# A linear-attention layer with a two-way maxout layer on one core: all operations and loads in another order, and 90 operations on other engines

## The chip, the cores and the metric

The kernel runs on one core of a Trainium2 chip. The core has TensorE (PE in the profile, its weight loads PEld), VectorE (DVE), ScalarE (ACT), GpSimd (POOL), and SyncE (SP), whose in-order queue issues all DMAs here. The engines run side by side, each works through its own instructions in order, and semaphores tie them together. The metric is the device time of one execution in microseconds.

## The reference

Inputs are r, k, v, w of 4 batches x 8 heads x 768 tokens x 48, u of 8 x 48, and three weight matrices.

```
state = 0
for t in range(768):                      # per batch and head, state is 48 x 48
    cur   = outer(u * k[t], v[t])
    y[t]  = r[t] @ (state + cur)
    state = w[t][:, None] * state + outer(k[t], v[t])
x   = y as 3072 tokens x 384
out = maximum(x @ w1, x @ w2) @ w_out     # 384 -> 1024 -> 384
```

## The kernel before

The work is cut into eight units. `UNITS` gives each (first batch, batches, segment of 256 tokens): units 0 to 3 are one batch each in segment 0, units 4 and 5 two batches each in segment 1, units 6 and 7 two batches each in segment 2. Each partition holds two neighbouring tokens, so a segment fills 128 partitions. The steps are small functions, named in the table by name, unit and further numbers:

- `load` brings w, r, k or v of a unit. `wp` multiplies the two decays of a token pair, `ln` takes the logarithm, `ex` sums it along tokens by a matmul with a triangle (units 3 to 7 with two half-precision parts, `hi` and `lo`), `mz` adds the unit's own part, `ie` and `e0` are exponentials of the sums (ScalarE).
- `rw` and `kw` are products with the second decay; `scale.n.0` makes the scaled r (`rp`), `scale.n.1` the scaled k (`kp`). `tr` transposes both on TensorE and `te` copies them to SBUF (units 0 to 4); `dt` transposes by DMA (units 5 to 7).
- `rk`, `ru`, `dg`, `dd`, `di` make the diagonal term with u. `sc` is the score matmul, `mk` merges it under a mask into M on VectorE, `vb` casts v, `ya` applies M to v, `yi` applies the state, `kv`, `st`, `sm`, `sb` update the state, `xe` copies y to SBUF as bf16.
- The maxout is max(h1, h2) = h2 + relu(h1 - h2). `wdiff` makes w1 - w2 once (three parts), `w2turn`, `w2take`, `wfold`, `wctake` fold w2 with w_out, `wocast` casts w_out. `gt` is the matmul with the difference, `rl` its relu (ScalarE or VectorE), `op` the output matmul, `oe` copies it out, `os` stores it.
- `hot` is eight matmuls on zeros each, of no use to the result; 48 of them stand in the front of both programs. `zero`, `ident`, `tri`, `mask` and `identb` fill constants.

What sets the order is one table, `ORDER`: a loop goes through it and calls the function of each word, so each engine's instructions stand in the table's order, and SyncE's queue too. Letters behind an @ choose the engine of a step (a for ScalarE, d for VectorE, p for GpSimd). `mul` (L176 on VectorE, L180 on GpSimd) makes one instruction of a product on VectorE and two halves on GpSimd; `copy` is L168. The tiles have few buffers (PSUM: four banks of tag G, two pairs of tag Y), which are handed on in the table's order.

```python
    for o in ORDER:
        o, _, e = o.partition("@")
        name, *a = o.split(".")
        a = [int(x) if x.isdigit() else x for x in a] + ([e] if e else [])
        if name in ops:
            ops[name](*a)
        else:
            unit[name](U[a[0]], *a[1:])
```

Of the kernel before, what the change touches and what calls it, by code (L numbers as in the profile page):

```python
# [59 lines left out]
rw.1.0@d wt.1.0 wload.1.2 ln.2.0 ex.2.0 vb.0.0@a we.0.1 scale.0.0.0.0@d zero.k.0@d kv.0  # L60
scale.0.0.0.1@d tr.0.0.1 dd.0@p mz.2.0 woload.0 we.1.0 ru.1.0@p kw.1.0@p row.2 w2turn.0.0 e0.1.0
scale.1.0.0.0@d st.0.0@a tr.0.0.0 te.0.0.1@a sc.0.0.1.1 sc.0.0.0.1 w2turn.0.1 dg.1 te.0.0.0@a
w2take.0.0@a wload.0.2 load.2.v scale.1.1.0.0@d dd.1@p sb.0.0@a wp.3.0@p tr.1.0.1 e0.2.0 st.0.1
te.1.0.1@a rk.2.0@d zero.M.2@p di.0.0@d ie.2.0 zero.M.0@p rw.2.0@d hot.8.1 wload.1.1 ru.2.0@d
kw.2.0@p scale.2.1.0.0@p sc.0.0.1.0 sc.0.0.0.0 mk.0.0.1.0 vb.1.0@a hot.8.4 mk.0.0.0.0 mk.0.0.1.1
mk.0.0.0.1 vb.1.1@a kv.1 scale.2.0.0.0@d tr.1.0.0 ln.3.0 te.1.0.0@a w2turn.2.1 wdiff.2@p sb.0.1@a
st.1.0@a sb.1.0@a di.1.0@d st.1.1 tr.2.0.0 w2take.0.1@a tr.2.0.1 te.2.0.1@a zero.v.0@d sc.1.0.1.0
w2turn.1.0 wload.0.0 wdiff.0@p w2take.1.0@a sc.1.0.0.0 mk.1.0.1.0 mk.1.0.0.0 sb.1.1@a w2take.2.1@d
w2turn.2.0 w2turn.1.1 w2take.2.0@a hi.3@a ya.0.0.1.0 vb.2.1@a ya.1.0.0.0 sm.0@p sm.1@p wload.0.1
wdiff.1@d ya.1.0.1.0 ya.0.0.0.1 load.3.r trih@a yi.1.0 yi.0.0 ya.0.0.0.0 woload.1 ya.0.0.1.1  # L70
xe.1.0@a xe.0.0@d load.3.k te.2.0.0@a gt.1.3 rl.1.3@a dg.2 rk.3.0@d lo.3@d dd.2@a gt.0.2 rl.0.2@a
wocast.1@p gt.1.1 w2take.1.1@d woload.3 gt.0.0 rw.3.0@p woload.2 rl.0.0@a gt.1.2 load.4.w.0 rl.1.2@a
vb.2.0@p ru.3.0@p gt.0.3 rl.0.3@a ex.3.0 wocast.3@d wocast.2@a wocast.0@a rl.1.1@a di.2.0@d
sc.2.0.1.0 mk.2.0.1.0 gt.0.1 mz.3.0 e0.3.0 kw.3.0@p gt.1.0 dg.3 sc.2.0.0.0 kv.2 st.2.0@a rl.0.1@a
wp.4.0@d ie.3.0 scale.3.0.0.0@d mk.2.0.0.0 wfold.2 sb.2.1@d wfold.0 dd.3@p ln.4.0 load.3.v st.2.1
wfold.1 sb.2.0@d vb.3.0@a wl.2 hi.4@a lo.4@d ya.2.0.0.0 load.4.r rl.1.0@a di.3.0@d vb.3.1@a row.3
ya.2.0.1.0 wctake.1@a we.2 load.4.k wctake.2@a rk.4.0@d wctake.0@a scale.3.1.0.0@p tr.3.0.0 ex.4.0
mz.4.0 tr.3.0.1 ex.4.1 mz.4.1 te.3.0.0@a kv.3 te.3.0.1@a st.3.0@a yi.2.0 xe.2.0@d ie.4.0 op.1.1
oe.1.1@a st.3.1 load.4.v e0.4.0 sb.3.0@a ru.4.0@d gt.2.0 load.5.w.0 rl.2.0@a sc.3.0.0.0 sc.3.0.1.0
vb.4.1@a gt.2.2 op.1.0 rk.4.1@p rw.4.0@d kw.4.0@d scale.4.0.0.0@d scale.4.1.1.0@d scale.4.1.0.0@p  # L80
e0.4.1 rl.2.2@a scale.4.0.1.0@d op.0.1 sb.3.1@a row.4 oe.1.0@a tr.4.1.0 te.4.1.0@a tr.4.1.1 vb.4.0@a
op.0.0 sm.2@p wl.3 mk.3.0.0.0 ya.3.0.0.0 mk.3.0.1.0 ya.3.0.1.0 yi.3.0 oe.0.1@d ru.4.1@p wp.5.0@p
we.3 sm.3@p te.4.1.1@a gt.2.1 xe.3.0@a dg.4 ln.5.0 oe.0.0@d tr.4.0.1 te.4.0.1@a gt.3.0 rl.3.0@a
rl.2.1@a hi.5@a dd.4@d load.5.k kv.4 di.4.0@d sc.4.1.1.0 load.5.r load.5.v rk.5.0@d gt.2.3 rl.2.3@a
gt.3.2 tr.4.0.0 di.4.1@d te.4.0.0@a mk.4.1.1.0 gt.3.3 st.4.0 st.4.1 os.1.0 rl.3.3@a gt.3.1 rl.3.1@a
ru.5.0@p sc.4.1.0.0 rk.5.1@p sc.4.0.0.0 load.6.r sb.4.0@a vb.5.1@a op.2.1 load.6.w.0 lo.5@d wl.4
ex.5.0 mk.4.0.0.0 os.0.0 sb.4.1@a mk.4.1.0.0 oe.2.1@a mz.5.0 e0.5.0 rw.5.0@p ex.5.1 sc.4.0.1.0
load.6.k ru.5.1@p mz.5.1 ya.4.0.0.0 scale.5.0.0.0@d op.2.0 rl.3.2@a op.3.0 mk.4.0.1.0 e0.5.1 os.1.1
scale.5.0.1.0@d dt.5.0.0 ya.4.0.1.0 dt.5.0.1 kw.5.0@d row.5 oe.3.0@d os.3.0 wp.6.0@p ie.5.0
ya.4.1.1.0 ya.4.1.0.0 oe.2.0@d yi.4.1 xe.4.1@d dg.5 dd.5@d scale.5.1.0.0@p di.5.0@d yi.4.0 xe.4.0@a  # L90
op.3.1 rk.6.0@d ln.6.0 hi.6@d gt.4.2 rl.4.2@a lo.6@d gt.4.5 scale.5.1.1.0@p rl.4.5@a os.2.1 gt.4.0
vb.5.0@a gt.4.7 rl.4.7@a we.4 sm.4@p gt.4.4 dt.5.1.0 gt.4.6 sc.5.0.1.0 mk.5.0.1.0 kv.5 oe.3.1@a
rl.4.6@a rl.4.0@a rl.4.4@a st.5.0 gt.4.1 rl.4.1@a sc.5.0.0.0 mk.5.0.0.0 gt.4.3 rl.4.3@a dt.5.1.1
rk.6.1@p st.5.1 ex.6.0 ru.6.1@p sb.5.1@a sb.5.0@a load.6.v os.0.1 vb.6.1@a mz.6.0 ex.6.1 op.4.3
load.7.w.0 load.7.k mz.6.1 e0.6.1 ie.6.0 kw.6.0@d e0.6.0 scale.6.1.1.0@p di.5.1@d sc.5.1.0.0
ya.5.0.1.0 rw.6.0@d ya.5.0.0.0 yi.5.0 xe.5.0@a vb.6.0@a scale.6.0.0.0@d op.4.2 wl.5 os.3.1
scale.6.1.0.0@p sc.5.1.1.0 oe.4.2@a op.4.0 oe.4.3@a oe.4.0@a mk.5.1.0.0 wp.7.0@p ya.5.1.0.0
mk.5.1.1.0 dt.6.0.0 ya.5.1.1.0 yi.5.1 kv.6 scale.6.0.1.0@d dt.6.0.1 xe.5.1@d st.6.0 dt.6.1.1 ln.7.0
op.4.1 sb.6.1@a sb.6.0@a oe.4.1@a ru.6.0@d dg.6 load.7.r dd.6@p gt.5.2 rl.5.2@a gt.5.4 di.6.1@d
gt.5.6 rl.5.6@a hi.7@a gt.5.0 dt.6.1.0 rl.5.0@a gt.5.3 di.6.0@d sc.6.1.1.0 rl.5.3@d rl.5.4@a  # L100
sc.6.1.0.0 gt.5.5 rl.5.5@a os.4.1 gt.5.7 rl.5.7@a rk.7.0@p lo.7@d gt.5.1 we.5 mk.6.1.1.0 rl.5.1@a
ex.7.0 op.5.1 op.5.2 oe.5.2@a sc.6.0.0.0 mk.6.1.0.0 ru.7.0@d mz.7.0 sc.6.0.1.0 mk.6.0.1.0 rk.7.1@p
ex.7.1 mk.6.0.0.0 e0.7.0 mz.7.1 op.5.3 oe.5.1@a load.7.v vb.7.1@a sm.5@p rw.7.0@p ie.7.0 os.2.0
ya.6.0.1.0 os.5.2 os.4.0 ya.6.1.0.0 ya.6.0.0.0 oe.5.3@a os.4.3 kw.7.0@p scale.7.1.1.0@p
scale.7.0.0.0@d ya.6.1.1.0 yi.6.0 xe.6.0@a scale.7.1.0.0@d dt.7.0.0 dt.7.1.0 yi.6.1 op.5.0 vb.7.0@p
xe.6.1@a gt.6.5 oe.5.0@d os.5.0 e0.7.1 gt.6.3 rl.6.3@a rl.6.5@a scale.7.0.1.0@d dt.7.1.1 gt.6.2
dt.7.0.1 os.4.2 kv.7 gt.6.6 gt.6.0 rl.6.6@a os.5.1 st.7.0 gt.6.1 rl.6.2@a ru.7.1@p dg.7 sb.7.1@a
gt.6.7 rl.6.7@a rl.6.0@d sc.7.0.0.0 rl.6.1@a dd.7@p di.7.0@d sc.7.0.1.0 mk.7.0.1.0 mk.7.0.0.0 gt.6.4
rl.6.4@a op.6.0 sc.7.1.0.0 sb.7.0@a sc.7.1.1.0 op.6.2 di.7.1@d mk.7.1.1.0 op.6.3 yi.7.1 mk.7.1.0.0
yi.7.0 ya.7.0.0.0 oe.6.2@a ya.7.1.0.0 ya.7.1.1.0 ya.7.0.1.0 xe.7.0@d op.6.1 oe.6.3@a os.6.3 oe.6.0@d  # L110
os.5.3 os.6.2 oe.6.1@d xe.7.1@a gt.7.1 rl.7.1@d gt.7.0 gt.7.6 os.6.0 rl.7.0@a gt.7.2 gt.7.3 rl.7.2@a
rl.7.6@a rl.7.3@a os.6.1 gt.7.4 rl.7.4@a gt.7.7 rl.7.7@d gt.7.5 rl.7.5@d op.7.0 op.7.1 oe.7.0@d
# [685 lines left out]
```

## Time and profile before

| | |
|---|---|
| time, median of 3 runs | 146.14 us (146.12 to 146.55) |
| span of the profiled execution | 147.2 us |
| TensorE busy | 136.8 us, 93% |
| VectorE busy | 116.9 us, 79% |
| ScalarE busy | 90.6 us, 62% |
| GpSimd busy | 90.0 us, 61% |
| read and written in HBM | 23.61 and 4.73 MB |

The span runs from the first to the last instruction of one profiled execution; no other time of that execution is given. Groups are told by line, engine, operation and tiles, with busy time, mean duration and the idle time just before; the chain of waits goes back from the last instruction to what released it. Line numbers of the changed kernel are one higher from the table on.

### The profile page before, as it was taken

What the parts mean: (1) busy time and instruction counts of PE and PEld (TensorE: products, weight loads), DVE (VectorE), ACT (ScalarE), POOL (GpSimd) and SP (SyncE); (2) the same over time, 40 slices, a digit from 0 to 9 for tenths busy, and PEclk for the clock granted to TensorE, in tenths of its full rate; (3) what the DMA queues carried; (4) which work ended last, traced back from release to release, by engine and by line L of the source; (5) the groups of instructions that cost most, each with busy time, mean ns of one, the idle gap of its engine ahead of it and who ended that gap; (6) DMA issues with size and microseconds to landing.
All of it is one profiled execution on the core that took longest, in us unless ns stands there. A gap on an engine that the chain in (4) does not pass through costs nothing.

```text
span 147.2 us, 5536 instructions
## 1 busy us (share of the span) xinstructions
PE 136.8 (93%) x2403; PEld 84.2 (57%) x2404; DVE 116.9 (79%) x162; ACT 90.6 (62%) x164; POOL 90.0 (61%) x106
## 2 busy tenths in 40 slices
...
GB/s 104 323 325 357 335 401 394 366 286 304 214 241 277 212 226 282 312 255 174 205 192 177 292 251 207 141 138 291 250 136 78 131 271 20 0 210 62 4 56 157
DMA packets 71186, 31.84 MB, mean 216 GB/s; under 512 B 66293, under 2 KB 70390, under 8 KB 71162
## 3 DMA queue, kind: packets, MB, share of 16 engines
...
q14 instruction: 5, 0.04, 0.2%
HBM read 23.61 MB, written 4.73 MB: 193 GB/s over the span
## 4 chain that ended last, share of the span: by engine, by line
PE 41%; DVE 35%; issue 6%; POOL 6%; DMA 4%; ACT 3%; SPq 2%; DVEq 0%; POOLq 0%; ACTq 0%
PE G L729 12%; DVE M L650 9%; PE G L706 8%; PE G L234 7%; PE G L725 5%; DVE rp L176 4%; DMA lv<-in_v_dram 4%; DVE rku L176 3%; DVE dg L502 3%; POOL kp L180 3%; DVE M L516 3%; PE Y L688 2%; SPq L582 2%; POOL rku L180 2%; PE Y L675 2%
## 5 line engine op out<-in xcount | busy, mean ns | idle before, releaser
L729 PE MATMUL G<-wo_sb,gT 128*128 128x384 bf16 x192 | 35.8, 331 | 0.0
L706 PE MATMUL G<-xT,wd_sb 128*128 128x256 bf16 (+1 forms) x192 | 34.4, 326 | 0.7 <-ACT xT L168 0.6
L650 DVE CAST_PREDICATED M<-mask,Y 128x1024 bf16<-128x1024 int32 (+1 forms) x26 | 28.6, 1131 | 2.8 <-PE Y L641 1.9
L717 ACT ACTIVATE gT<-G 128x512 bf16<-128x512 f32 x43 | 24.5, 601 | 9.8 <-PE G L706 9.6
L729 PEld LDWEIGHTS <-gT 128*128 128x128 bf16 x192 | 19.0, 99 | 12.6 <-issue 0.3
L706 PEld LDWEIGHTS <-wd_sb 128*128 128x128 bf16 x192 | 17.9, 98 | 12.6 <-DVE wd_sb L176 0.6
L180 POOL TENSOR_TENSOR kp<-lk,iE 128x384 bf16<-128x384 f32 x16 | 17.1, 1096 | 9.3 <-DVE lk L176 4.2
L725 PE MATMUL G<-wc_sb,xT 128*128 128x384 bf16 x72 | 15.7, 327 | 0.0
L180 POOL TENSOR_TENSOR rku<-rku,u_b 128x384 f32<-128x384 f32 x14 | 14.5, 1053 | 2.0 <-DVE rku L176 2.0
L234 PE MATMUL G<-S_b 128*128 128x512 bf16 x47 | 13.6, 442 | 1.8 <-DVE S_b L263 1.8
L168 ACT COPY RK<-G 128x1024 bf16<-128x1024 bf16 x12 | 12.1, 1019 | 4.7 <-PE G L565 4.7
L168 ACT COPY osb<-G 128x384 f32<-128x384 f32 x7 | 3.4, 479 | 15.9 <-PE G L729 12.6
L180 POOL TENSOR_TENSOR rku<-lr,lk 128x384 f32<-128x384 f32 x8 | 10.9, 1393 | 2.5 <-DMA lk<-in_k_dram 1.7
L641 PE MATMUL Y<-RK 48*64 48x128 bf16 x384 | 9.0, 220 | 2.6 <-DVE M L650 2.4
L502 DVE TENSOR_REDUCE dg<-rku 128x16 f32<-128x768 f32 x12 | 11.0, 945 | 0.1
L641 PEld LDWEIGHTS <-RK 48*64 48x64 bf16 x384 | 6.2, 106 | 7.8 <-issue 6.7
L168 ACT CAST xT<-Y 128x768 bf16<-128x768 f32 x7 | 7.0, 1025 | 5.3 <-PE Y L675 4.0
L168 ACT CAST S_b<-S_f 64x768 bf16<-64x768 f32 (+1 forms) x14 | 8.7, 624 | 2.3 <-DVE S_f L612 2.0
L176 DVE TENSOR_TENSOR rp<-lr,G 128x768 bf16<-128x768 f32 (+2 forms) x11 | 8.8, 799 | 1.4 <-ACT G L436 1.4
L234 PEld LDWEIGHTS <-S_b 128*128 128x128 bf16 x48 | 5.1, 112 | 8.3 <-issue 3.3
L516 DVE TENSOR_TENSOR M<-identq,gd 128x512 int32<-128x512 int32 x12 | 9.2, 778 | 0.4 <-POOL gd L168 0.3
L168 DVE CAST xT<-Y 128x768 bf16<-128x768 f32 x5 | 5.1, 1017 | 5.5 <-PE Y L688 3.2
...
## 6 DMA issues: line engine op xcount, KB each, us to landing
...
```

Source lines behind the costliest of these rows:

```text
L168: (nc.scalar.copy if e == "a" else nc.vector.tensor_copy if e == "d" else nc.gpsimd.tensor_copy)(o, i)
L176: op(o, a, b)
L180: op(o[:, g], a[:, g], b[:, g])
L234: nc.tensor.matmul(t, zz[:, 0:P], zz[:, 0:512], start=True, stop=True)
L502: nc.vector.reduce_sum(s.dg[:, b].rearrange("p i h -> p h i"), s.rku[:, b], axis=AX.X)
L516: (nc.vector if en == "d" else nc.gpsimd).tensor_tensor(out=o, in0=m, in1=g.unsqueeze(3).to_broadcast([P, 2, H, Q // 2]), op=ALU.bitwise_and)
L641: nc.tensor.matmul(t[q * Q:(q + 1) * Q, e, p * P:(p + 1) * P].rearrange("s (i g) -> s i g", i=2), s.kT[d, b, j, y * n + p, q, :], s.rT[d, ...
L650: nc.vector.copy_predicated(t[:, :, 2 * n * y:2 * n * (y + 1)].rearrange("s i (p e) g -> s p e i g", e=2), mask[:, j].bitcast(I32).unsquee ...
L706: nc.tensor.matmul(t[:, m * n * P:(m + 1) * n * P].rearrange("c (b t) -> c b t", t=P), wd_sb[:, ko, fo * P:(fo + 1) * P], s.xT[:, 0:n, ko, :],
L717: nc.scalar.activation(o, i, AF.Relu)
L725: nc.tensor.matmul(t[:, 0:HD], s.xT[:, a, ko, :], wc_sb[:, ko, :], start=(ko == 0), stop=False)
L729: nc.tensor.matmul(t[:, 0:HD], s.gT[:, c:c + P], wo_sb[:, f, :], start=False, stop=(f == FO - 1))
```

## The change

Only `ORDER` changes: the same 652 words in another order, and 90 of them with another letter. From GpSimd 25 operations go to VectorE and 6 to ScalarE; from VectorE 18 go to GpSimd and 21 to ScalarE; from ScalarE 18 go to VectorE and 2 to GpSimd. The first words, before and after:

```diff
-ident zero.s.1@p identq@a load.0.k load.0.r zero.m@p identb@p u zero.s.0@d zero.r@d rk.0.0@d
-load.0.w.1 load.0.w.0 wp.0.0@d hot.8.2 hot.8.3 load.2.w.0 zero.v.1@d wp.0.1@d mask ln.0.0 tri
...
+ident zero.o@p zero.M.0@p zero.s.0@d zero.M.2@p hot.8.3 load.0.w.0 wp.0.0@d ln.0.0 tri ex.0.0
+identq@a zero.m@p identb@d load.0.w.1 wp.0.1@d zero.k.0@d zero.k.1@d zero.r@d ln.0.1 load.0.r
...
```

Three places follow. The first is VectorE up to the weight difference `wd_sb`, without which the first `gt` cannot run; `M0` and `M1` are the masks of units 0 and 1, `rku` the product for the diagonal, T the state's sum, `gT` here a buffer of the weight loads. Before:

```order
L650 COPY_PREDICATED M0_80<-mask_71,Y_389 128x4x2x64 x2
L650 COPY_PREDICATED M0_80<-mask_71,Y_319 128x4x2x64 x2
L176 TENSOR_TENSOR rp0_73<-lr_220,G_237 128x16x48
L516 TENSOR_TENSOR M1_81<-identq_79,gd_288 128x2x256
L615 TENSOR_TENSOR T_363<-Y_421,S_f_84 128x192
L254 MEMSET vp0_76 128x8x2x8
L255 MEMSET vp0_76 128x8x2x8
L650 COPY_PREDICATED M1_81<-mask_71,Y_501 128x8x2x64
L650 COPY_PREDICATED M1_81<-mask_71,Y_528 128x8x2x64
L168 CAST wb_548<-G_466 128x512
L176 TENSOR_TENSOR wd_sb_86<-gT_383 128x1024
```

The same place on VectorE in the changed program:

```order
L651 COPY_PREDICATED M0_80<-mask_71,Y_338 128x4x2x64 x2
L616 TENSOR_TENSOR T_326<-Y_401,S_f_84 128x192
L651 COPY_PREDICATED M1_81<-mask_71,Y_435 128x8x2x64
L651 COPY_PREDICATED M1_81<-mask_71,Y_463 128x8x2x64
L651 COPY_PREDICATED M0_80<-mask_71,Y_502 128x4x2x64 x2
L177 TENSOR_TENSOR rp0_73<-lr_310,G_242 128x16x48
L177 TENSOR_TENSOR wd_sb_86<-gT_355 128x1024
L177 TENSOR_TENSOR wd_sb_86<-gT_390 128x1024
```

Unit 1's masks moved between those of unit 0, and a second part of the weight difference (`wdiff.0`) came to VectorE from GpSimd.

The second place is ScalarE around the end of unit 5's attention; `vp1_77<-lv` is `vb.6` (the cast of unit 6's v), `G<-G` is `e0.6`, `iE` is `ie.6`, `xT` is `xe.5`, `gT` is a relief `rl.5`. Before:

```order
L168 CAST S_b_85<-S_f_84 64x2x8x48 x2
L168 CAST vp1_77<-lv_2032 128x8x2x48
L436 ACTIVATE G_2038<-G_2038 128x384
L460 ACTIVATE iE_2061<-MZ_83 128x768
L436 ACTIVATE G_2025<-G_2025 128x384
L168 CAST xT_2175<-Y_2085 128x6x2x64
L168 CAST vp1_77<-lv_2032 128x8x2x48
```

And in the changed program:

```order
L461 ACTIVATE iE_2082<-MZ_83 128x768
L169 COPY wb_2102<-G_2070 128x384
L437 ACTIVATE G_2064<-G_2064 128x384
L437 ACTIVATE G_2032<-G_2032 128x384
L169 COPY osb_2268<-G_2122 128x384
L169 CAST xT_2321<-Y_2202 128x6x2x64
L169 COPY wb_2351<-G_2329 128x384
L718 ACTIVATE gT_2353<-G_2342 128x512
L169 CAST vp1_77<-lv_2000 128x8x2x48
L718 ACTIVATE gT_2353<-G_2355 128x512
L169 CAST vp1_77<-lv_2000 128x8x2x48
```

Both casts of unit 6's v moved behind the exponentials, behind `xe.5` and behind the first relief of unit 5.

The third place is SyncE's queue from the transposes of unit 5 on (`DMA_TRANSPOSE`, the step `dt.5`); `lv` is v of unit 6 and the next `lw`, `lk`, `lr` are of unit 7. Before:

```order
L582 DMA_TRANSPOSE RK_1678<-kp1_75 128x8x128 x2
L372 DMA lv_2032<-in_v_dram 128x8x96 x2
L743 DMA out_0_dram<-osb_1328 128x384
L372 DMA lw_2053<-in_w_dram 128x8x96 x2
L372 DMA lk_2056<-in_k_dram 128x8x96 x2
L478 DMA WL_2191<-row_1714 128x8x1
L743 DMA out_0_dram<-wb_1986 128x384
L582 DMA_TRANSPOSE RK_2269<-rp0_73 128x8x128 x2
L582 DMA_TRANSPOSE RK_2269<-kp0_74 128x8x128
L372 DMA lr_2386<-in_r_dram 128x8x96 x2
```

And in the changed program:

```order
L583 DMA_TRANSPOSE RK_1779<-kp1_75 128x8x128
L744 DMA out_0_dram<-osb_1103 128x384
L744 DMA out_0_dram<-osb_1858 128x384
L473 DMA row_1861<-MZ_83 1x1024
L744 DMA out_0_dram<-wb_1855 128x384
L373 DMA lk_1884<-in_k_dram 128x8x96 x2
L373 DMA lr_1925<-in_r_dram 128x8x96 x2
L373 DMA lv_2000<-in_v_dram 128x8x96 x2
L744 DMA out_0_dram<-wb_1745 128x384
L744 DMA out_0_dram<-osb_2268 128x384
L583 DMA_TRANSPOSE RK_2271<-rp0_73 128x8x128
```

Unit 7's r moved from behind three of unit 6's transposes to ahead of them all, its w to a place before unit 5's transposes, and unit 6's v from just behind unit 5's transposes to behind three stores and unit 7's k and r.

More of the change, by code (lines that the diff above doesn't have):

```diff
@@ L60 @@
[L60 to L112, printed above, removed]
@@ new lines @@
+dd.0@a ie.0.0 we.0.1 rw.1.0@d mz.1.0 rk.1.0@d wp.2.0@p scale.0.1.0.1@p ln.2.0 ie.1.0 ru.1.0@d
+hot.8.4 tr.0.0.1 e0.1.0 te.0.0.1@a load.0.v vb.0.1@a wt.1.0 kw.1.0@d zero.v.0@p we.1.0 ex.2.0 mz.2.0
+e0.2.0 ie.2.0 dg.1 scale.1.0.0.0@d hot.8.1 hot.8.2 vb.1.0@a dd.1@a vb.1.1@a scale.1.1.0.0@p kv.1
+di.1.0@d st.1.0@a sb.1.0@a load.2.r load.2.k rk.2.0@d scale.0.1.0.0@d di.0.0@d mask st.1.1 tr.1.0.0
+te.1.0.0@a sc.0.0.1.1 sc.0.0.0.1 wload.1.0 w2turn.0.0 wload.1.2 zero.v.1@p tr.1.0.1 row.2 rw.2.0@p
+mk.0.0.1.1 tr.0.0.0 kw.2.0@p vb.0.0@a wload.1.1 wload.0.2 mk.0.0.0.1 load.2.v scale.2.1.0.0@p
```

58 lines of the change are left out of this document (53 added, 5 removed).

## Prediction

> **What bounds the kernel now.** I read the page first, then sums by stretch, then the chain that ended last, then the timeline around the places that the chain names.
>
> ```profile
> span 147.2 us, 5536 instructions
> ...
> PE 136.8 (93%) x2403; PEld 84.2 (57%) x2404; DVE 116.9 (79%) x162; ACT 90.6 (62%) x164; POOL 90.0 (61%) x106
> ```
>
> TensorE is busy for 93% of the span; 10.4 us are left. The table by stretch tells where they lie.
>
> ```profile
> core 0: us, PE busy (x) PEld busy (x) DVE busy (x) ACT busy (x) POOL busy (x), PEclk, DMA share, GB/s
> 0.00:33.00 33.00, 28.79 (x425) 17.03 (x427) 27.61 (x50) 19.89 (x43) 27.95 (x46) 1.00 1.03 322
> 33.00:77.00 44.00, 43.86 (x858) 30.48 (x858) 43.27 (x58) 35.37 (x63) 34.73 (x35) 1.00 0.98 241
> 77.00:97.00 20.00, 17.59 (x397) 10.32 (x395) 15.74 (x20) 12.63 (x22) 11.16 (x11) 0.91 0.96 208
> 97.00:127.00 30.00, 29.76 (x470) 16.80 (x468) 24.52 (x28) 18.06 (x31) 16.19 (x16) 1.00 0.65 156
> 127.00:147.20 20.20, 16.83 (x259) 9.62 (x257) 5.71 (x9) 4.64 (x8) 0.00 (x0) 0.99 0.25 89
> ```
>
> Four stages show. In 0:33 TensorE's count is filled up with `hot` matmuls, so the front is not bound by it: VectorE sets its length. In 33:77 TensorE (43.86 of 44) and VectorE (43.27) are both full. In 77:97 TensorE loses 2.41 us, and its clock stands at 0.91. In 97:127 it is full again. The last stretch is the tail of unit 7, with the last store. So two stages can give something: the front, and 77:97. The chain names what went wrong in the latter.
>
> ```profile
> 72.91 3.91 POOL kp L180 x4
> 76.82 1.08 SPq L582
> ...
> 79.33 0.57 SPq L372
> ...
> 79.96 6.14 DMA lv<-in_v_dram
> ...
> 86.17 0.04 ACT vp L168
> ...
> 86.91 0.47 ACT G L436
> 87.39 0.76 ACT iE L460
> 88.14 0.39 ACT G L436
> ...
> 88.55 0.95 DVE rp L176
> 89.51 1.15 DVE M L650
> ...
> 90.70 0.42 PE Y L641 x16
> ...
> 98.03 3.24 PE G L706 x15
> ...
> 131.50 5.18 PE G L706 x24
> ```
>
> GpSimd scales k of unit 5 late (72.91 to 76.82). SyncE's queue has `dt.5.1.0` and `dt.5.1.1` (L582) waiting for that, and behind them `load.6.v` (L372), which lands at 86.10. ScalarE's in-order `vb.6.1` waits for it with `e0.6.1`, `ie.6.0`, `e0.6.0` queued behind; VectorE's `scale.6.0.0.0` waits for `e0.6.0`, `mk.5.1.0.0` stands behind that, and TensorE waits for the mask.
>
> ```profile
> 90.70 0.42 PE L641 MATMUL Y<-RK 48*64 48x128 bf16 x16 [1.94 <-DVE M L650]
> ...
> 91.70:93.70 2.00, 2.00 (x17) 0.81 (x22) 1.55 (x2) 0.00 (x0) 2.00 (x3) 0.61 0.84 170
> 93.70:96.00 2.30, 2.30 (x121) 1.92 (x120) 0.47 (x1) 1.22 (x2) 0.30 (x1) 0.59 0.66 126
> 96.00:98.00 2.00, 2.00 (x22) 1.22 (x17) 1.97 (x4) 0.97 (x2) 0.00 (x0) 1.00 1.30 98
> ```
>
> The wait itself is 1.94 us, and after it the granted clock is 0.61 and 0.59 over 4.3 us: lost 2.00 x 0.39 + 2.30 x 0.41 = 1.72 us. Together 3.66.
>
> **The change, part by part.** No instruction is added or dropped; 90 operations go to another engine, and all stand in another order.
>
> *The stall at 86.* In the new ScalarE row the two casts of `lv` of unit 6 stand behind the first reliefs of unit 5, and both exponentials `e0.6` stand ahead of them. So the late load holds up nothing until unit 5's `gt` runs (98.03 before). Nor is a load of unit 7 behind `dt.6` any longer, apart from `load.7.v`. I take the whole 3.66 off; the ends are 0 (the wait returns elsewhere, a rival) and 3.66 plus the rest of TensorE's idle time in 33:127, 0.14 + 0.47 + 0.24 = 0.85. I take 0.4 of that 0.85, half: 4.1 in all.
>
> [...]
>
> *The front.*
>
> ```profile
> 5.50 0.96 DVE L176 TENSOR_TENSOR rku<-lr,lk 128x768 f32<-128x768 f32 x1 [3.49 <-DMA lr<-in_r_dram]
> ...
> 31.25 1.42 DVE L176 TENSOR_TENSOR wd_sb<-gT 128x1024 bf16<-128x1024 f32 x1
> ...
> 33.11 1.03 PE L706 MATMUL G<-xT,wd_sb 128*128 128x256 bf16 x8 [0.60 <-ACT xT L168]
> ```
>
> VectorE stands still until 5.50 for the second load, and is then nearly full up to `wdiff.1` (31.25 to 32.67). Now the first load is half of unit 0's w, 192 KB where two loads of 384 KB had to come before. The 576 KB of difference take 1.8 us at the 322 GB/s of 0:33; since `identb` behind it waits for GpSimd's fills, I estimate a start 1.5 earlier. What it has to do up to `wdiff.1` is about the same. Added: `ru.1.0`, `scale.0.1.0.0`, `wdiff.0` at 1.42, two products and three fills; dropped or put later: `ru.2.0`, `scale.1.1.0.0`, `wp.2.0`, `rw.2.0`, `rw.0.0`, `w2take.2.1`, three fills; my sum over their timeline durations is -0.2. The weight loads are asked for behind 12 unit loads where it was 13 and one of w_out, so they come no later. `xe.1.0`, which ended last before (0.60), now stands behind unit 1's own masks, which come ahead of two of unit 0's. I take 1.5; the ends are 0 (TensorE or a load holds it) and 2.7 (1.8, the 0.60 and some 0.3 of fewer meetings with GpSimd).
>
> *The dense part: what VectorE must now do.* Prices per operation:
>
> ```profile
> L176 DVE TENSOR_TENSOR rku<-rku,u_b 128x768 f32<-128x768 f32 x5 | 5.3, 1061 | 0.0
> L180 POOL TENSOR_TENSOR rku<-rku,u_b 128x384 f32<-128x384 f32 x14 | 14.5, 1053 | 2.0 <-DVE rku L176 2.0
> L719 DVE TENSOR_SCALAR gT<-G 128x512 bf16<-128x512 f32 x5 | 3.4, 690 | 3.3 <-PE G L706 3.2
> L717 ACT ACTIVATE gT<-G 128x512 bf16<-128x512 f32 x43 | 24.5, 601 | 9.8 <-PE G L706 9.6
> L168 DVE CAST xT<-Y 128x768 bf16<-128x768 f32 x5 | 5.1, 1017 | 5.5 <-PE Y L688 3.2 <-PE Y L675 2.3
> ```
>
> A 128x768 product costs GpSimd two halves of 1.05 and VectorE 0.95 undisturbed (1.06 in the mean). Between `wdiff.1` and the last mask of unit 7, VectorE takes over from GpSimd 13 such products (12.4) and four small ones (1.7), and `ru.2.0` (0.9) now falls here. From ScalarE it takes four reliefs at 0.69, three `xe` at 1.02, and `te.2.0.0`, `oe.3.1`, `hi.7`, `vb.7.1`, `trih` and two `sb`, 9.9 in all; no row has a `te` or a wide `sb` on VectorE, and the nearest, the 1.02 of `xe` and half of it, bound each, so 9.9 lies between 8.9 and 10.4. It gives GpSimd 11 products (11.4 by their timeline durations), and ScalarE `xe` x4, `oe` x4, two reliefs, two casts and the like (10.8). Net +2.7 us (1.7 to 3.2). Its busy time there rises from 83.5 (43.27 + 15.74 + 24.52) to 86.2, while GpSimd over the whole program gives up 14 products of 2.1, `wdiff.0` and several casts and fills for 12 products and a few small ones, so some 12 us less, and ScalarE gains about 2 and stays under 65%.
>
> TensorE's work there is the same, so the stretch can shrink from 94.0 (33 to 127) by the 4.1, to 89.9, with VectorE idle for 3.7 where it was 10.5. That needs VectorE 96% busy; in 33:77 it reached 98%. Whatever more idleness it has lands on the path one for one. From 77 to 127 it had 9.7 idle (4.26 and 5.48); I allow 1.5 us of new waits, with ends 0 and 9.
>
> *The tail.* Last mask, `yi`, `xe`, eight `gt`, four `op`: the same matmuls, one `op` of unit 6 as cover as before. Two stores of unit 5 stand just ahead of the last store, under 1.8 us of the last `op`. Cost 0 (ends 0 and +0.5, where their bytes are in the way).
>
> *Sum.* 147.2 - 1.5 - 4.1 + 1.5 = 143.1 as profiled. The profiled execution lies 1.06 above the median 146.14, so 142.0 us.
>
> **The rivals.** *The wait comes back in another place.* SyncE still has `dt.5.1.1` ahead of three stores, `load.7.k`, `load.7.r` and `load.6.v`, all in order; so 6.v can be later than it was. Against it: unit 5's `gt`, ahead of the cast, came at 98.0. If it or a like wait strikes, it costs the clock too: 1.2 us beyond my 1.5, and 1.72, gives 144.9.
>
> *The order does not matter.* Every stage is limited by the sum of an engine's work, what the front gains is lost at the next full engine, and the change is worth nothing: 146.1. For it: three engines near full in 33:77. Against: 3.66 us are one chain of waits, which is gone.
>
> *VectorE held up by GpSimd: slower.*
>
> ```profile
> 26.16 2.96 POOL L180 TENSOR_TENSOR wd_sb<-wst 128x512 bf16<-128x512 f32 x2
> ...
> 26.48 1.50 DVE L516 TENSOR_TENSOR M<-identq,gd 128x512 int32<-128x512 int32 x1
> ...
> L516 DVE TENSOR_TENSOR M<-identq,gd 128x512 int32<-128x512 int32 x12 | 9.2, 778 | 0.4 <-POOL gd L168 0.3
> ```
>
> An operation of VectorE with two inputs in SBUF, asked for while GpSimd works, ran 1.50 where its group's mean is 0.78. The kernel now has some 5 more such operations on VectorE, and VectorE has no slack. If every second of about 40 in the dense part loses 0.4, half of this excess of 0.72, that is 8 us, of which 2.0 are already in the durations: 148.0. It decides from 4.6 us of such loss on (146.58 - 142.0). Against it: GpSimd has 12 us less to do, so fewer meetings. [...]
>
> **How the numbers follow.** About 0.3% (0.44 us) is what a measurement here can tell. The forecast 142.0 has 0.52, with its own range from 139.9 (front 2.7, all of the 0.85, new waits 1.0) to 143.8; the returning wait 0.25; no effect 0.08; slower 0.15. Faster 0.77, same 0.08, slower 0.15. The range 139.5 to 146.3 leaves out the slower case and a few hundredths below.
>
> **What would show it.** In the new profile: `wd_sb` L177's last product on VectorE ending near 31.2 and TensorE's first L707 near 31.5; no wait over 1 us between 77 and 97 and a clock of 1.00 there; unit 5's first `gt` near 92 and the run of unit 7's near 127 (131.50 before); VectorE's busy share in the dense part at 94 to 97%. Wrong it would be if VectorE's two-input products stood over 1.2 us in the mean, if the clock halved anywhere, or if a store or `dt` kept a load of unit 5 or 6 behind its use.

## The result, and the profile after

The changed kernel takes 159.05 us in the median of 4 runs (156.76 to 159.56), the kernel before 146.34 beside it. Ratios here and below compare undisturbed executions alone (of the changed kernel 156.76 and 158.57 us), and the profiled one, 159.56 us, is the longest of the four, so the rows below show the loss at its fullest. The ratio is 1.076, with an interval of 1.066 to 1.085: slower by 7.6%. I had forecast 142.0 us.

The page of the changed kernel first: span, busy time of the engines, and the clock in 40 slices.

```profile
span 157.8 us, 5532 instructions
...
PE 141.2 (90%) x2403; PEld 86.5 (55%) x2404; DVE 126.8 (80%) x164; ACT 92.9 (59%) x171; POOL 80.4 (51%) x93
...
PEclk9959999699999999999965999969999999999999
```

VectorE has 9.9 us more to do than before (116.9) and GpSimd 9.6 less (90.0). The same table by stretch as in the prediction:

```profile
core 0: us, PE busy (x) PEld busy (x) DVE busy (x) ACT busy (x) POOL busy (x), PEclk, DMA share, GB/s
0.00:33.00 33.00, 28.43 (x343) 16.25 (x352) 24.95 (x45) 18.01 (x41) 22.69 (x41) 0.90 0.96 284
33.00:77.00 44.00, 41.62 (x887) 30.20 (x886) 43.17 (x54) 38.71 (x68) 27.32 (x26) 1.00 0.92 233
77.00:97.00 20.00, 16.28 (x222) 8.45 (x205) 15.33 (x19) 10.65 (x19) 11.45 (x11) 0.83 1.07 249
97.00:127.00 30.00, 27.77 (x586) 16.23 (x586) 28.07 (x31) 15.61 (x29) 18.71 (x16) 0.94 0.61 132
127.00:157.80 30.80, 27.10 (x399) 15.34 (x397) 15.32 (x20) 9.91 (x18) 0.26 (x2) 1.00 0.44 106
```

The stretch 77:97, from which I took 4.1 us, has become worse: TensorE loses 3.72 us in it, where it lost 2.41, at a clock of 0.83. To see where the time went, the span is better cut at VectorE's own marks: the end of `wdiff.1` and the end of the last mask of unit 7. Before:

```profile
32.70:126.50 93.80, 90.71 (x1718) 57.30 (x1718) 83.83 (x104) 66.36 (x115) 62.38 (x62) 0.98 0.88 208
```

After:

```profile
0.00:35.10 35.10, 30.53 (x444) 17.88 (x446) 27.02 (x46) 20.11 (x45) 23.02 (x42) 0.90 0.96 285
35.10:137.90 102.80, 94.47 (x1748) 59.40 (x1746) 95.10 (x112) 66.81 (x117) 57.40 (x52) 0.95 0.83 191
137.90:157.80 19.90, 16.20 (x239) 9.20 (x222) 4.71 (x7) 5.97 (x11) 0.00 (x0) 1.00 0.30 111
```

So the front grew by 2.4, the dense part by 9.0, and the tail shrank by 0.8. In the dense part VectorE's work (third figure) grew by 11.3 us, from 83.83 to 95.10. And TensorE stands still there for reasons that no row of before had shown:

```profile
75.84 1.29 PE L689 MATMUL Y<-M,vp 64*32 64x128 bf16 x128
77.07 0.57 PE L676 MATMUL Y<-RK,S_b 128*32 128x128 bf16 x27
81.36 0.83 PE L676 MATMUL Y<-RK,S_b 128*32 128x128 bf16 x21 [3.72 <-issue]
82.13 1.14 PE L726 MATMUL G<-wc_sb,xT 128*128 128x384 bf16 x3
83.06 2.77 PE L730 MATMUL G<-wo_sb,gT 128*128 128x384 bf16 x8
...
100.73 0.68 PE L676 MATMUL Y<-RK,S_b 128*32 128x128 bf16 x34
103.37 0.46 PE L676 MATMUL Y<-RK,S_b 128*32 128x128 bf16 x14 [1.95 <-issue]
```

It stops in the middle of `yi` (L676), whose two halves have 24 matmuls each: 27 are done, 21 follow 3.72 us later, and nothing in the profile releases them ("issue"). A half can wait for data at its first matmul, not at its fourth; at 101 it is the eleventh. Behind it the eight matmuls of an `op` take 2.77 us, where 1.46 is usual: the granted clock is 0.50 from 79.69 to 86.52. The view of the DMA queues has the other half of the story:

```profile
## 3 DMA queue, kind: packets, MB, share of 16 engines
q1 hardware_dynamic: 71162, 31.49, 78.6%
q8 instruction: 19, 0.31, 0.8%
```

Queue q8 is marked as instruction: 19 packets of 16 KB. TensorE has 2403 + 2404 matmuls and weight loads, 253 for each packet. Counted in the trace, TensorE stands at its instructions 441 (1.47 us, at 26.34), 951 (1.01), 2486 (3.94), 3253 (2.17) and 4531 (0.62), counted from one start to the next, of which the rows show the idle part; the distances are 510, 1535, 767 and 1278, which is 2, 6, 3 and 5 times 255.5. The profile names a releaser only for the one at 951 (0.74 us of idle time, a relief of ScalarE), which stands here by its place. At each of the five, a packet of q8 has landed 1.3 to 1.5 us before it goes on (79.87 and 81.36; 102.06 and 103.37). My reading of these counts, which the first kernels below test: a packet holds some 256 of TensorE's instructions, called a page from here on, and at each of the five TensorE had worked a page off before the next one was there. `ya` of a unit is 128 matmuls with a weight load each, a whole page in 1.3 us; in the new order `ya` and `yi` of units 4 and 5 stand in one piece, 352 instructions in 1.8 us. In before two `op` lay between their parts. The stalls are not of this one execution: a kernel below with the same page ends (reductions made lighter) has both again, 2.58 and 2.04 us.

### The profile page after: what moved, and what is told of

It reads as the page before. It is cut to its first block, busy times and chain, and to the rows that moved or that the text cites. A ratio compares the mean times of both kernels' runs of the same rounds, so it can differ in the third digit from the quotient of the medians.

```text
span 157.8 us, 5532 instructions
## 1 busy us (share of the span) xinstructions
PE 141.2 (90%) x2403; PEld 86.5 (55%) x2404; DVE 126.8 (80%) x164; ACT 92.9 (59%) x171; POOL 80.4 (51%) x93
## 4 chain that ended last, share of the span: by engine, by line
PE 81%; issue 6%; ACT 5%; DVE 4%; DMA 2%; ACTq 0%
PE G L730 20%; PE G L707 19%; PE G L726 9%; PE G L235 6%; PE Y L689 5%; PE Y L642 4%; PE Y L676 3%; PE G L566 3%; PE G L319 3%; PE Y L597 2%; PE G L308 2%; DMA lw<-in_w_dram 2%; DVE M L651 1%; PE G L467 1%; ACT gT L718 1%
## 5 line engine op out<-in xcount | busy, mean ns | idle before, releaser
L730 PE MATMUL G<-wo_sb,gT 128*128 128x384 bf16 x192 | 37.6, 342 | 0.0
L181 POOL TENSOR_TENSOR kp<-lk,iE 128x384 bf16<-128x384 f32 x12 | 11.8, 1004 | 12.2 <-issue 6.3
L169 ACT COPY wb<-G 128x384 f32<-128x384 f32 x9 | 4.3, 477 | 16.6 <-PE G L730 16.6
L169 ACT COPY osb<-G 128x384 f32<-128x384 f32 x11 | 5.3, 480 | 12.7 <-PE G L730 12.6
L517 DVE TENSOR_TENSOR M<-identq,gd 128x512 int32<-128x512 int32 x12 | 11.5, 972 | 0.2
L676 PE MATMUL Y<-RK,S_b 128*32 128x128 bf16 x240 | 5.7, 229 | 5.7 <-issue 5.7
L177 DVE TENSOR_TENSOR rku<-rku,u_b 128x768 f32<-128x768 f32 x9 | 10.2, 1132 | 0.6 <-ACT u_b L169 0.5
L181 POOL TENSOR_TENSOR rku<-lr,lk 128x384 f32<-128x384 f32 x6 | 8.1, 1371 | 4.3 <-DVE dg L503 4.3
L177 POOL TENSOR_TENSOR S_f<-T,W 128x192 f32<-128x192 f32 (+1 forms) x5 | 4.9, 984 | 10.3 <-ACT W L489 10.3
L169 ACT CAST vp<-lv 128x384 bf16<-128x384 f32 (+1 forms) x15 | 9.9, 658 | 0.0
```

The costliest lines, as they stand in the source:

```text
L169: (nc.scalar.copy if e == "a" else nc.vector.tensor_copy if e == "d" else nc.gpsimd.tensor_copy)(o, i)
L177: op(o, a, b)
L181: op(o[:, g], a[:, g], b[:, g])
L517: (nc.vector if en == "d" else nc.gpsimd).tensor_tensor(out=o, in0=m, in1=g.unsqueeze(3).to_broadcast([P, 2, H, Q // 2]), op=ALU.bitwise_and)
L730: nc.tensor.matmul(t[:, 0:HD], s.gT[:, c:c + P], wo_sb[:, f, :], start=False, stop=(f == FO - 1))
```

## The experiments

All of them are the kernel before or after with words of `ORDER` or single lines changed. Line numbers in their rows differ by up to 3. The expectations use short labels: a_pads is the kernel after with its page ends moved in three `op`, a_pads_lite the same with lighter reductions, a_relief the same as a_pads with four operations more on ScalarE.

**Pages: the kernel before, with its page ends moved.** A block of `hot` gets tiny matmuls at the start of the program, and nothing else changes. For half a page:

```diff
-hot.8.2
+hot.5.2.67     # 5 large matmuls, then 67 of 128x32 weights and 128 columns
```

> The order of before, untouched. Only the first block of `hot` matmuls is changed: 5 of its 8 large ones and then 67 tiny ones (128x32 weights, 128 columns), so that TensorE has 128 instructions more ahead of everything else, half a page of 256. Theory (TensorE's instructions come in pages of 256; a page that is worked off faster than the next one can be fetched leaves TensorE standing): the page ends move 128 instructions forward. In before's trace the pages then cut would last 1.84 us (ending at 32.2, first gt), 1.31 us (111.8, in ya/yi of unit 6) and 1.59 us (129.9, behind ya of unit 7), where 3.5 to 5 us are needed from one page's start to the next one's use; so stalls of about 2 us each at these three places that have no releaser, each with some half clock behind it: 152 to 157 us against 146.3. Rival (what held after up is data: late loads, stores, ScalarE's or VectorE's row): nothing of that is changed, 146 to 147.5 us.

And for a whole page, `hot.8.3` in the same way besides:

> As the half-page kernel, but the first two blocks of `hot` are changed in this way: 256 instructions more, one whole page. Theory of pages: the page ends fall on the same instructions as in before, so no new stall: 146 to 148 us (the front may lose up to 1.5 to the tiny matmuls at half clock), although it has more instructions than the half-page kernel, which comes out 5 us or more slower. Rival (data): the same 146 to 148; if the tiny matmuls themselves did harm, this one would be the slower of the two.

Half a page: 152.72 us, ratio 1.033 (1.025 to 1.040). A whole page: 147.43, ratio 1.004 (1.000 to 1.007). So 128 instructions more cost 3.3%, 4.8 us of 146.74, and 256 more cost 0.4%, 0.6 us: both as the theory of pages has it, and the first beyond the rival's 147.5. In the half-page kernel:

```profile
32.40 0.35 PE L689 MATMUL Y<-M,vp 64*32 64x128 bf16 x16
34.85 0.35 PE L689 MATMUL Y<-M,vp 64*32 64x128 bf16 x16 [2.11 <-issue]
...
112.75 0.29 PE L676 MATMUL Y<-RK,S_b 128*32 128x128 bf16 x7
113.68 0.79 PE L676 MATMUL Y<-RK,S_b 128*32 128x128 bf16 x41 [0.63 <-issue]
```

In the whole-page kernel the same words run through:

```profile
33.08 0.43 PE L689 MATMUL Y<-M,vp 64*32 64x128 bf16 x32
```

Of the three places named, two stalled near where I put them (32.2 and 111.8); the third stalled at 131.7 for 1.9, 1.6 of it idle time ahead of an `op`. The half clock that I had counted in did not come: the granted clock is 1.00 in each stretch up to 127 us, and no slice of the page stands under 0.9. So half a page in front brings stalls and 4.8 us to the order of before, whose own trace shows none.

**Pages: the kernel after.** First `ya` and `yi` pulled apart in units 4 and 5, with the `op` between them:

```diff
-op.3.1 ... op.3.0 ... ya.4.0.0.0 ya.4.0.1.0 ya.4.1.0.0 ...
+ya.4.0.0.0 ya.4.0.1.0 op.3.1 ... op.3.0 ... ya.4.1.0.0 ...
-op.4.0 ya.5.0.0.0 ya.5.0.1.0 ... yi.5.0 yi.5.1
+ya.5.0.0.0 ya.5.0.1.0 yi.5.0 op.4.0 ... yi.5.1
```

> The order of after with five words moved on TensorE: ya.4.0.0.0 and ya.4.0.1.0 go ahead of op.3.1 (two op, 22 instructions and 3.7 us, then stand between them and the rest of unit 4's ya and yi), and ya.5.0.0.0, ya.5.0.1.0, yi.5.0 go ahead of op.4.0. All other engines' rows stay. Theory of pages: the two stalls inside yi of units 4 and 5 (3.94 and 2.17 us, with the half clock behind them 10.4 us in all) go or shrink to under 1 us: 148.7 us, between 147 and 151. Rival (data): the two halves wait for the same masks, casts and loads as before the move, so 157 us or more.

158.02 us, ratio 1.077 (1.072 to 1.082): no gain, and the rival's range. The two stalls are gone, but the edit made a wait of its own, since `ya` needs the PSUM pair that the masks of the other half free:

```profile
74.56 1.07 PE L686 MATMUL Y<-M,vp 64*32 64x128 bf16 x64 [2.46 <-DVE M L648]
```

So it tells nothing on the price of the stalls. Then the order of after untouched, 112 instructions more in front (`hot.8.3` to `hot.5.3.59`):

> The order of after, untouched, with 112 more TensorE instructions in its first block of `hot` (5 large and 59 tiny ones in place of 8 large). Theory of pages: the page ends move 112 instructions forward. The stalls in yi of units 4 and 5 (3.94 and 2.17 us) go; new short pages come at the end of ya of unit 6 (page of 1.41 us: about 2 us of stall), behind ya of unit 7 (3.56), and small ones near 33, 61 and 94 (3.1 each, up to 1 us of stall each). 151 to 156 us, and the places of the stalls are others. Rival (data): the same waits at the same operations, 158 to 160 us.

157.05 us, ratio 1.060 (1.055 to 1.065). The stalls went where the page ends went (1.05 us at 29.2, 1.99 at 33.1, 0.79 at 64.8, 1.06 at 100.2), and those in `yi` of units 4 and 5 are gone. The ratio is 1.6 points lower than after's, some 2 us, but the executions of the two kernels overlap (155.09 to 160.15 here), and the theory of pages asked for 3 to 8: the median lies between the two theories. The third kernel has tiny matmuls in three `op` alone, which clear all page stalls behind 40 us and bring no new wait of data in their place:

```diff
-op.2.0 ... op.5.0 ... op.6.3
+op.2.0.88 ... op.5.0.20 ... op.6.3.60
```

> The kernel after, with tiny matmuls put in at the start of three op words only to move the page ends of TensorE's instructions: 88 in op.2.0, 20 in op.5.0, 60 in op.6.3 (about 1.7 us of TensorE in all, overwritten by the op itself). No order, engine or wait is changed. Theory 1 (page stalls are on the path): the stalls of 3.94, 2.17 and 0.62 us in yi and ya of units 4, 5 and 7 go, with the half clock behind the first two: 148 to 151 us. Theory 2 (VectorE's row is the bound and the stalls lie mostly beside it): only what VectorE itself waited for there goes, 3.9 us for xe.4.0 and about 1 for xe.5.0, less 0.5 for the tiny matmuls: 153.5 to 156 us. Theory 3 (the stalls cost nothing): 158 to 160.

158.72 us, ratio 1.074 (1.064 to 1.085). `yi` of unit 4 runs through, and unit 5's first `gt` starts at 102.3 (107.1 in after), but the masks of unit 6 end at 119.2 (121.0): the gain is given back. The time is in the range of the third theory, but not for its reason: the stalls did cost, and something else took their place. The row of VectorE says what:

```profile
84.97 1.58 DVE L174 TENSOR_TENSOR kp<-lk,iE 128x768 bf16<-128x768 f32 x1
86.47 1.80 DVE L500 TENSOR_REDUCE dg<-rku 128x16 f32<-128x768 f32 x2
...
105.96 1.36 DVE L200 TENSOR_SCALAR wst<-lg 128x768 f16<-128x768 f32 x1
107.35 1.64 DVE L411 SCALAR_TENSOR_TENSOR wst<-lg,wst 128x768 f16<-128x768 f32 x1
```

From 84 to 119 it works without a pause longer than 0.3 us. Several operations there are far longer than their kind: L200 (`hi`) took 0.552 in before, the product into `kp` is 0.95 where undisturbed.

**VectorE: order or engines?** The order of after with all 90 operations on their old engines; the order of before with the new ones; the order of after with the 43 changes between VectorE and GpSimd undone:

> The order of after, with the engine of every one of the 90 operations as it was in before. Where we stand: from the end of `wdiff.1` to the last mask VectorE is busy 83.8 of 93.8 us in before and 95.1 of 102.8 in after, and removing page stalls left the time of after nearly as it was. Theory (VectorE's row is too long: the 90 changes put 11 us more on it in that part, where I had worked out 2.7): with the old engines it is busy about 84 to 86 again and the kernel takes 146 to 151 us. Rival (the order itself, with its in-order waits and page stalls, costs it): 155 us or more, since the order is that of after.

> The order of before, with the engine of every one of the 90 operations as in after. Theory (VectorE's row): VectorE busy for about 94 in the dense part, 153 to 158 us. Rival (the order costs it): 146 to 149 us.

> The order of after; of its changes of engine only the 43 between VectorE and GpSimd are undone (25 go back to GpSimd, 18 to VectorE), those with ScalarE stay. By the durations in after's and before's traces these 43 put 16.7 us on VectorE and took 11.4 off it in the dense part, 5.2 of the net 9.4. Theory (VectorE's row): busy some 5 to 7 us less there, 151 to 154 us. Rival (the order): no change, 157 us or more. [...]

176.78, 167.39 and 174.64 us, ratios 1.203, 1.142 and 1.188. The theories of VectorE's row missed by far in all three; the rivals missed too (149 at most) or had only named a lower end (155 and 157), and nothing foresaw such times. With the old engines in the new order VectorE stands for 55 of 177 us; GpSimd waits 14.3 us for ScalarE's exponential and ScalarE 12.7 for the first matmuls of the MLP. Rows and engines belong together: an operation that is put on another engine at the same place of the order finds another queue ahead of it. So such mixtures cannot tell which half of a change costs.

**VectorE made lighter, nothing else.** The reduction for the diagonal sums a third of the columns:

```diff
-nc.vector.reduce_sum(s.dg[:, b]..., s.rku[:, b], axis=AX.X)
+nc.vector.reduce_sum(s.dg[:, b]..., s.rku[:, b][..., 0:16], axis=AX.X)
```

> The kernel after, but each of the 12 reductions `dg` (0.946 us in the mean) sums only 16 of 48 columns of a head, so the diagonal term is left incomplete. Nothing else changes. VectorE has some 0.55 us less per reduction, 10 of them in the dense part: 5.5 us. Theory VectorE (its row is the bound in the dense part: busy 95.1 of 102.8): 4 to 6 us faster, 153 to 155 us. Theory TensorE (pages, half clock, order): under 1.5 us faster, 157 to 159.

> The same cut in before: each `dg` sums 16 of 48 columns. VectorE is busy 83.8 of 93.8 us in the dense part there, TensorE 90.7. Theory VectorE: it bounds less here, 1 to 3 us faster than before: 143.5 to 145.5. If VectorE bounds before as much as after, 141 to 142.5; if it does not bound at all, 146 to 147.

> After with both edits of before: the tiny matmuls in three op that move the page ends, and the 12 reductions cut to 16 of 48 columns (so the diagonal term is incomplete). Alone they gave nothing (158.7) and 2 us (157.1). Theory A (two bounds one behind the other: page stalls of TensorE up to unit 5's gt, then VectorE's full row from 84 to 119; whichever is taken away, the other one sets the masks of unit 6): together clearly more than the sum, 5 to 8 us, 151 to 154 us. Theory B (neither of the two bounds the kernel): the sum, 156.5 to 158.

Each reduction fell from 0.946 to 0.414 us. In after that gave 157.08, ratio 1.071 (1.065 to 1.076): by the ratios 0.7 us, theory TensorE. In before it gave 145.48, ratio 0.993 (0.990 to 0.996), 1 us, the small end of the first theory there. Together with the moved page ends it gave 152.31, ratio 1.036 (1.031 to 1.041). In points of before's time: moved ends 0.1, light reductions 0.5, both 4.0. Each alone is inside the interval of after's own ratio (1.066 to 1.085), both together are far outside. That is theory A: two bounds stand one behind the other, TensorE's page stalls up to unit 5's `gt` and VectorE's row from there to the masks of unit 6. Whichever goes, the other one sets when unit 6 can start. The dense part of the three (moved ends, light, both):

```profile
36.20:138.10 101.90, 94.42 (x1949) 60.43 (x1941) 94.30 (x111) 66.99 (x117) 57.88 (x52) 0.98 0.86 193
```
```profile
34.50:135.30 100.80, 92.25 (x1773) 58.62 (x1760) 90.20 (x112) 67.01 (x117) 57.48 (x52) 0.98 0.85 195
```
```profile
34.10:131.40 97.30, 92.82 (x1949) 59.93 (x1948) 90.04 (x112) 66.97 (x118) 58.65 (x52) 1.00 0.90 202
```

The same with the full computation: moved ends, and `hi.7`, `dd.6`, `sb.6.1` and `dd.5` on ScalarE at the same places of the order.

> After with the tiny matmuls in three op that move the page ends, and four operations of VectorE of units 5 and 6 given to ScalarE at the same places of the order: hi.7 (1.36 us on VectorE), sb.6.1 (1.26), dd.6 (0.97) and dd.5 (0.19). Nothing is left out. Theory (two bounds in a row, as a_pads_lite had it: with the page stalls gone, what VectorE's row loses between 84 and 119 comes off the time): 3 to 3.8 us less than the 158.7 of a_pads, 155 us, between 154 and 156.5. Rival (ScalarE's in-order row cannot take them without holding reliefs up): 157.5 or more.

153.25 us, ratio 1.037 (1.032 to 1.042), somewhat better than expected. Of the kernels tried, this is the fastest with the changed order that computes everything.

**Does VectorE's row get long by meeting GpSimd?**

> After with the tiny matmuls in three op, and with ten in-place products of GpSimd left out in units 4 to 7 (rw.4, kw.4, kw.5, ru.5.1, rw.6, ru.6.0, kw.6, ru.7.0, rw.7, kw.7: 20 halves and wholes, some 20 us of GpSimd), so the result lacks these factors. VectorE's own row is unchanged. Theory L (VectorE's row is long because its operations meet GpSimd's: hi.7 1.36 for 0.55, rk.6.0 1.75 for 0.95, di 1.37 for 0.68): VectorE's busy time in the dense part falls by 3 to 5 us from 94.2 and the kernel takes 152 to 155. Theory N (the number of operations on VectorE is what counts): VectorE's busy time stays within 1.5 us, 157 to 159.

152.47 us, ratio 1.041 (1.035 to 1.046). VectorE's busy time in the dense part fell from 94.30 to 91.68 with its own row untouched, a little less than the 3 that theory L asked for and well over N's 1.5. The time is no such test, since GpSimd's own row became shorter as well (34.12 for 57.88 in the dense part):

```profile
34.40:132.10 97.70, 92.50 (x1935) 59.50 (x1925) 91.68 (x112) 66.84 (x117) 34.12 (x32) 1.00 0.92 201
```

`di` came down from 978 to 897 ns in the mean, the product with `u_b` from 1132 to 1055, the wide cast of the state from 789 to 555. In after itself the meeting can be read off, VectorE's two rows first and GpSimd's behind them:

```profile
88.67 1.38 DVE L517 TENSOR_TENSOR M<-identq,gd 128x512 int32<-128x512 int32 x1
89.97 1.75 DVE L177 TENSOR_TENSOR rku<-lr,lk 128x768 f32<-128x768 f32 x1
```
```profile
88.47 2.44 POOL L181 TENSOR_TENSOR lg<-lw 128x384 f32<-128x384 f32 x2
90.86 1.72 POOL L181 TENSOR_TENSOR rku<-lr,lk 128x384 f32<-128x384 f32 x1
```

VectorE's product was asked for at 89.97 with GpSimd's half running until 90.91; it took 1.75, which is 0.95 and about the rest of that half. `hi.7`, 0.55 us in before (`hi.6`), shows the same, VectorE's row again ahead of GpSimd's:

```profile
106.85 1.35 DVE L203 TENSOR_SCALAR wst<-lg 128x768 f16<-128x768 f32 x1
```
```profile
106.02 3.04 POOL L181 TENSOR_TENSOR rku<-lr,lk 128x384 f32<-128x384 f32 x2 [4.34 <-DVE dg L503]
```

Held against the shortest of their kind, 16 operations of VectorE in the dense part of after took over 0.1 us too long, 9.2 us together, and each overlaps an instruction of GpSimd; in before it was 8 operations with 2.8 us. All of them have their inputs in SBUF. None of the 56 operations that read PSUM is among them, and none of the reductions, whose mean stays at 0.94 to 0.95 in every kernel that does them whole.

**The front.**

> The kernel after with fewer filling matmuls ahead of ex.1.0 and ex.2.0: hot.8.5 is cut from 8 to 3, hot.8.0 and hot.8.4 to 2 each; 17 tiny matmuls in hot.8.1 make up for the number of instructions, so that the page ends of later units stay. Theory (TensorE's row, not VectorE, holds up the front of after: VectorE waited 1.06 us for mz.1.0 and 0.91 for mz.2.0 behind hot blocks, one of them at half clock): mz.2.0 comes 1.5 to 2.5 us earlier than 18.8, wdiff.1 1 to 2.5 earlier, the kernel takes 156 to 157.8 us. Rival (the front is held up by VectorE meeting GpSimd, or by loads): no change, 158.5 to 159.5; if fewer hot matmuls leave the clock halved for longer, it is slower.

159.69 us, ratio 1.078 (1.069 to 1.087): no gain, and no loss that can be told from after's 1.076. In the front the rival's last sentence came true: with fewer large matmuls the clock was 0.61 from 8 to 16 and 0.50 from 16 to 22 (0.79 and 1.00 in after), and `mz.2.0` came at 20.9 for 18.8.

> The kernel a_relief (after, page ends moved in three op, four operations of VectorE given to ScalarE), with 62 instructions more in TensorE's first block of `hot` (5 large and 34 tiny matmuls for 8 large) and 62 fewer in op.2.0, so that only the page ends ahead of unit 4 move. They then fall near instructions 380, 636 and 891 of after's own count and no longer on 441 (1.47 us of stall in the front, with half clock behind it) and 951 (1.01). Theory (the page stall in the front is what makes it longer than before's): wdiff.1 starts at 32 to 33 (33.9 in after, 34.5 in a_relief) and the kernel takes 151 to 152.3 us, 1 to 2 less than a_relief. Rival (the front's loss is TensorE's row, half clock or loads, whatever the page ends): wdiff.1 at 33.5 to 35 and 152.8 to 154.

Three executions took 156.75, 157.37 and 160.15 us, a fourth 740.23 for which there is no explanation, so no ratio is formed. The forecast failed: `wdiff.1` started at 33.4, but the page ends that were moved off 441 and 951 gave stalls of 0.78 at 32.4 and 2.80 at 38.4:

```profile
35.24 0.34 PE L563 MATMUL G<-identb,rp 128*128 128x128 bf16 x3
38.39 0.27 PE L563 MATMUL G<-identb,rp 128*128 128x128 bf16 x1 [2.80 <-issue]
```

I had reckoned with 3.5 to 5 us from one page's start to the next one's use; here it was 6.0 (32.4 to 38.4), in a stretch where the page has the DMA engines at 0.9 or more (31 to 39 us).

**My first term by itself.** In before, one word of VectorE's row:

```diff
-scale.6.0.0.0@d ... mk.5.1.0.0
+mk.5.1.0.0 scale.6.0.0.0@d ...
```

> Before with one word moved: VectorE does mk.5.1.0.0 ahead of scale.6.0.0.0 and not behind it. So the mask no longer stands behind e0.6.0, which stood behind vb.6.1 and the late load.6.v; the PSUM pair that sc.5.1.1.0 waits for comes free 2 us earlier. This is the part of the change that my prediction took 3.66 us from. Theory (the wait of 1.94 us and the half clock behind it, 1.72, are on the path and nothing else is late there): 142.5 to 143.5 us. Rival (the next wait is close behind: load.7.r, dt.6, GpSimd's row): 144.5 to 146. Rival (worth nothing): 146 to 147.

> Before with the moved mask mk.5.1.0.0 (145.43 by itself) and four fills of VectorE (zero.v.1, zero.v.2, zero.k.0, zero.v.0; 0.31 + 0.31 + 0.27 + 0.3 = 1.2 us) put at the start of its row, where it stands idle from 2.01 to 5.50 for the second load. Theory (VectorE's row sets the length of the front, up to wdiff.1): 0.8 to 1.2 us less, 144.2 to 144.7. Rival (TensorE's row, loads or GpSimd set it): 145.2 to 145.7; if the fills hold GpSimd's first ones up, slower than that.

145.43 us, ratio 0.992 (0.989 to 0.995), and 145.19, ratio 0.992 (0.989 to 0.994). The wait at 90 is gone and the clock is 1.00, but it was worth 1.2 us and not 3.66, the range of the first rival; the four fills moved out of the front gave nothing that can be told from zero (`wdiff.1` at 31.56 for 31.50). Both are faster than before and than after.

## Why the prediction was wrong

*The forecast against the trace.* I had 143.1 as profiled: a front to about 31.2, a dense part of 91.2 (93.8 - 4.1 + 1.5), a tail of 20.7. It came to 35.1, 102.8 and 19.9. The dense part failed by 11.6, the front by 3.9; the tail's zero was right within 0.8.

*"Net +2.7 us (1.7 to 3.2)" for VectorE: the step that failed most.* VectorE's busy time in the dense part grew by 11.3. By the rows, the 32 operations that came to it (with `ru.2.0`) took 29.3 us, where I had 24.9; the 25 that left had taken 21.2, where I had 22.2; the rest, those it had in both, grew by 3.5, where I had 0. (These are sums of durations, 11.6 in all; neighbours overlap a little, so the busy time grew by 11.3.) The list was right and the durations were those of an engine left alone. `hi.7` took 1.35 for 0.55, `ru.4.1` 1.64 and `ru.7.1` 1.59 for 0.95, `dd.6` 0.99 for about 0.2, `di` 0.97 in the mean for 0.78:

```profile
L517 DVE TENSOR_TENSOR M<-identq,gd 128x512 int32<-128x512 int32 x12 | 11.5, 972 | 0.2
```

Of the 8.6 us by which the +2.7 was short, 6.4 stand in the traces as meetings with GpSimd (9.2 less the 2.8 of before). That is my third rival: the meetings and their size (8 us, 2 of them in the durations already) stood in the prediction, and I gave it 0.15, since GpSimd had 12 us less to do and so "fewer meetings". Its time, 148.0, was far too low even so, since nothing in it allowed for page stalls. GpSimd did have 9.6 less; the meetings cost more all the same. Its test on record ("two-input products over 1.2 us in the mean") did not strike: those with `u_b` stand at 1.13. The loss lay in `di`, casts and single operations. The other test, "if the clock halved anywhere", did strike (0.50 from 79.69 to 86.52, for one).

*"The stall at 86: -4.1".* The wait of data is gone, as I said; a wait of another kind took the place. My first rival, the returning wait, named loads, a store or `dt`; none of them is the cause. What stood there was TensorE's own row of instructions, which no row of before had shown: 3.72 us, and a clock of 0.83 over the stretch. And the 3.66 were never to be had. I set the profiled span of 147.2 beside a median time of 146.14; the runs since list both, and a time is the span and some 1.8 us (146.68 with 144.9). So the profiled execution was some 2.3 us longer than the usual one, which is about what the term was too large by, and 143.1 as profiled would have been a time of 144.9, not 142.0. Nor does half clock follow every wait of such a length (last section). With a whole page in front the same wait is shorter and has no half clock behind it:

```profile
90.64 0.42 PE L642 MATMUL Y<-RK 48*64 48x128 bf16 x16 [0.93 <-DVE M L651]
```

*"The front: -1.5 (0 to 2.7)".* VectorE does start earlier, 3.53 for 5.50, and `mz.2.0` is 2.4 later, 18.80 for 16.40. Between them VectorE waits for TensorE's in-order row, where `wt.0.1` and blocks of `hot`, one of them at half clock (0.50 from 8.01 to 11.42), stand ahead of `ex.1.0` and `ex.2.0`:

```profile
DVE MZ L441 <- PE G L399: 2.0, 2, 1.1
```
```profile
8.43 5.08 PE L235 MATMUL G<-S_b 128*128 128x512 bf16 x16
13.54 0.61 PE L467 MATMUL G<-MZ 128*128 128x1 f32 x4
14.01 0.89 PE L399 MATMUL G<-lg,tri 128*128 128x384 f32 x2
```

then a page end takes 1.47 at 26.34. "VectorE sets its length" was the wrong reading of a front that TensorE's count fills with `hot`: the four fills taken out of it in before gave nothing.

*The allowance "+1.5 of new waits, ends 0 and 9"* held only within its ends: VectorE's idle time in the dense part is 7.7, where I had 4.7, so the new waits are 4.5 and not 1.5; 3.85 of the idle time is the wait for `xe.4.0` behind the page stall. But this is not what the stalls alone cost: without them the time stayed, since VectorE's row was next.

*How far the cause is shown.* Shown: pages cost time (half against whole), the two bounds in a row (neither alone, both together, and again with the full computation), and that meetings with GpSimd lengthen VectorE's row (its products left out). What the meetings cost in time is not shown by itself. Of the 7.6% that the change lost, moved page ends and four operations off VectorE take back 3.9 points. The remaining 3.7 points, some 5.4 us, are not settled. The front has a part in it: `wdiff.1` ended 1.4 to 4.5 us later than before's 32.7 in every kernel with after's rows but one (a_shift, 32.75). Page ends (1.47 us at 26.34), the half clock (0.90 over 0:33) and TensorE's order all stand there, and no experiment told them apart. The trace of a_shift (after with 112 instructions more in front) has a clock of 1.00 in every stretch from 0 to 34 us, which speaks against the order as such: the same rows can end there as early as before's.
